# Seven half-size products for eight in the layers of six experts, with gathers, buffers and small steps in another order

## The chip, the cores and the metric

The kernel runs on one core of a Trainium2 chip. A core has a matrix engine (TensorE, in the profile PE for the products and PEld for the loading of their stationary operand), two engines for elementwise work (VectorE, DVE, and ScalarE, ACT), a programmable engine (GpSimd, POOL) that here issues the gathers and scatters, and a queue engine (SyncE, SP) that issues the plain transfers. Operands lie in the on-chip memory SBUF, results of TensorE in PSUM[...].

The metric is the device time of one launch in microseconds. The profile is a further, separately recorded execution.

## The reference

Two blocks are computed one after the other. The first is attention over 4 batches, 8 heads, 768 positions of 64 numbers, in which a query sees only the keys of the same hash bucket:

```python
q_bits = (np.einsum('bhsd,dk->bhsk', q, proj) > 0); k_bits = ...          # 6 bits
mask = q_bucket[:, :, :, None] == k_bucket[:, :, None, :]
scores = np.where(mask, q @ k.T / sqrt(64), -1e9)
attn = softmax(scores);  x = attn @ v          # then rearranged to 3072 tokens x 512
```

The second sends each of the 3072 tokens to one of 8 experts, the one with the largest cosine, and weighs the result with its softmax probability:

```python
expert_idx = np.argmax(logits, axis=1)                       # cosine of x and expert_emb
for e in range(8):                                            # D = 512, F = 1024
    h = np.maximum(x[mask] @ w1[e], 0.0)                      # first layer
    out[mask] = gate_w[mask, None] * (h @ w2[e])              # second layer
```

All inputs and outputs are float32. Nothing is rounded to a shorter type on the way, save the hash bits and masks, which are exact there.

## The kernel before

Attention goes in groups of three units; a unit is one block of 128 keys against 384 queries of two heads. TensorE makes the scores, ScalarE the exponentials, VectorE adds up the denominators, and TensorE multiplies with the values. Sixteen pairs of heads (`pr`) follow one another, four to a batch. After a pair, its result is divided by the denominators, squared for the norm and stored to a table `xd` in the main memory. The division and the sum of squares are partly on GpSimd:

```python
def add_squares(pr, rp):
    ...
    nc.scalar.activation(t[:], xs(b)[:, j], ACT.Square)
    if j > 0:
        nc.gpsimd.tensor_tensor(out=ssq[b][:], in0=ssq[b][:], in1=t[:], op=ALU.add)

def scale(pr):
    ...                                     # reciprocal, and its way through memory to rz
    nc.gpsimd.tensor_tensor(out=x, in0=x, in1=rz[:].rearrange("p s n -> p (s n)"), op=ALU.mult)
```

The last pair has no time for that way through memory. Its denominators are spread to all rows by a product with ones, and the reciprocal is taken of 384 columns:

```python
nc.tensor.matmul(ps[h * D : (h + 1) * D, 0, 0:SH], lhsT=ones[:, 0:D], rhs=acc[pr, s][:, h, :], ...)
...
nc.vector.reciprocal(out=z[:, s], in_=z[:, s])
```

After each batch the router counts its tokens into slots: each expert has three tiles of 128 tokens (`KT = 3`), and what does not fit goes to further tiles at the end. Two experts (`EARLY = 2`) get two tiles filled from the first three batches alone, so that TensorE has their 256 tokens to work on while the last batch is routed. The rows of a tile are gathered from `xd` by four indirect transfers and turned by VectorE:

```python
def fetch(pos, t, n, width=N + 1):
    ...
            for g in range(NQ):
                nc.gpsimd.indirect_dma_start(out=xg[:, g, :], ..., in_=xd[0 : width * NQ, :], ...)

def turn(parts, at):
    ...
        nc.vector.transpose(x[:, :, i * P : (i + 1) * P]..., xg[:]...)
```

The two layers of an expert (P = 128, ND = 4 blocks of the 512, NF = 8 blocks of the 1024):

```python
def hidden(i, xt, n, fs=range(NF)):
    for f in fs:
        ph = ps_h()
        for d in range(ND):
            nc.tensor.matmul(ph[:, 0:n], lhsT=w1s[i][:, d, f * P : (f + 1) * P], rhs=xt[:, d, 0:n], ...)
        nc.scalar.activation(ht[:, f, 0:n], ph[:, 0:n], ACT.Relu)

def second(i, j):
    py = ps_y()
    for f in range(NF):
        nc.tensor.matmul(py[:], lhsT=ht[:, f, j * P : (j + 1) * P], rhs=w2s[i][:, f, :], ...)
    return py

def result(i, tiles):
    for j, gate, src in tiles:
        send(weigh(second(i, j), gate), src)        # VectorE scales, GpSimd scatters
```

Each matmul of float32 stands in the profile as two instructions with a weight load each. The loop over the six experts with three tiles:

```python
for e in range(EARLY, E):
    i = e % NW                                       # NW = 3 sets of weights
    x, tiles = nxt
    if e == EARLY:
        late = [...]                                 # third tiles of the two early experts
    elif e + 1 < E:
        nxt = rows_of(e + 1)                         # 12 gathers, 3 turns, 3 gate gathers
    ...
    hidden(i, x, KT * P)
    ...
    bring1(i, e + NW)                                # next first-layer weights, 2 MB
    result(i, tiles)
    if e == EARLY:
        nxt = rows_of(e + 1)
        for o in range(EARLY):
            hidden(o, late[o][0], P); bring1(o, NW + o)
            result(o, late[o][1]);    bring2(o, NW + o)
        bring1(i, e + NW); bring2(i, e + NW)
    elif e + NW < E:
        bring2(i, e + NW)
```

After the loop follow the tiles beyond three, here two of 128 tokens.

Of the kernel before, what the change touches and what calls it, by code (L numbers as in the profile page):

```python
# [26 lines left out]
def kernel(  # L27
# [320 lines left out]
    NW = 3  # L348
# [6 lines left out]
    def bring1(i, e, **kw):  # L355
        nc.sync.dma_start(w1s[i][:], w1[bass.ds(e, 1)].rearrange("o (c p) f -> p (o c) f", p=P), **kw)
# [9 lines left out]
    def bring2(i, e, **kw):  # L366
        nc.sync.dma_start(w2s[i][:], w2[bass.ds(e, 1)].rearrange("o (c p) m -> p (o c) m", p=P), **kw)
# [5 lines left out]
    def fetch(pos, t, n, width=N + 1):  # L373
        parts = []
        for i in range(n):
            xg = xgs[taken[0] % len(xgs)]
            taken[0] += 1
            for g in range(NQ):
                nc.gpsimd.indirect_dma_start(  # L379
                    out=xg[:, g, :], out_offset=None, in_=xd[0 : width * NQ, :],  # L380
                    in_offset=bass.IndirectOffsetOnAxis(ap=pos[:, t + i, g : g + 1], axis=0))
            parts.append(xg)
        return parts
# [21 lines left out]
    ssq, lts = {}, {}  # L405


    def add_squares(pr, rp):
        b, j = pairs[pr]
        if j == 0:  # L410
            ssq[b] = ssq_
        t = ssq_ if j == 0 else rp.tile([P, S], F32, name="xsq", tag="junk", bufs=2)
        nc.scalar.activation(t[:], xs(b)[:, j], ACT.Square)  # L413
        if j > 0:
            nc.gpsimd.tensor_tensor(out=ssq[b][:], in0=ssq[b][:], in1=t[:], op=ALU.add)  # L415
# [13 lines left out]
    with ExitStack() as at:  # L429
# [52 lines left out]
        ld, feat, acc, av, zcs = {}, {}, {}, {}, {}  # L482
# [120 lines left out]
        def scale(pr):  # L603
# [5 lines left out]
            for h in range(2):  # L609
                nc.sync.dma_start(rz[h * D : (h + 1) * D],  # L610
                                  zd[pr].rearrange("(s h) n -> h s n", h=2)[h].unsqueeze(0).broadcast_to([D, 2, SH]))
            x = xs(b)[:, j]
            nc.gpsimd.tensor_tensor(out=x, in0=x, in1=rz[:].rearrange("p s n -> p (s n)"), op=ALU.mult)  # L613
# [11 lines left out]

        def scale_last(pr, s):
            b, j = pairs[pr]
            if s == 0:
                zcs[pr] = op.tile([P, 2, SH], F32, name="zl", tag="rz", bufs=1)
            z = zcs[pr]  # L630
            ps = banks()
            for h in range(2):
                nc.tensor.matmul(ps[h * D : (h + 1) * D, 0, 0:SH], lhsT=ones[:, 0:D], rhs=acc[pr, s][:, h, :],
                                 start=True, stop=True)
            nc.scalar.activation(z[:, s], ps[:, 0, 0:SH], ACT.Copy, bias=TINY * S)

        def scaled_last(pr, s):
            b, j = pairs[pr]
            z = zcs[pr]
            nc.vector.reciprocal(out=z[:, s], in_=z[:, s])  # L640
            x = xs(b)[:, j, s * SH : (s + 1) * SH]
            nc.vector.tensor_tensor(out=x, in0=x, in1=z[:, s], op=ALU.mult)
            nc.vector.tensor_tensor(out=z[:, s], in0=x, in1=x, op=ALU.mult)
# [55 lines left out]
        for u0 in range(0, U + G, G):  # L699
# [4 lines left out]
            if end and j == 2 and g == 3:  # L704
                run(99)
                listed = lists(slots, src[0][:], NS, rp)
            for u in range(u0, u0 + G):
                if u < U:
                    scores(u)
            for u in range(u0 - G, u0):  # L710
                if 0 <= u < U:
                    attend(u)
            if end and j == 2 and g == 3:
# [4 lines left out]
            if g == 0:  # L718
                if pr > 0:
                    sums(pr - 1)  # L720
                if j == 2 and end:
                    begin(b, spare(2 * E * NC))
# [7 lines left out]
            elif g == 1:  # L730
                prep_features(pr + 1, 1)
                if pr > 0:
# [18 lines left out]
            elif g == 2:  # L751
                prep_bits(pr + 1)
                if pr > 1:
                    store(pr - 2)
                if j == 2 and end:
                    run(99)
                    fill(b, spare(4 * NS))
                if j == 2 and b >= 0:
# [3 lines left out]
            else:  # L762
                if pr == 1:
# [3 lines left out]
                if j == 1 and b >= 0:  # L767
                    route(b, turn_logits(lts.pop(b), banks()[:, 0], rp), rp)
                if j == 3 and b >= 0 and not end:
                    run(99)  # L770
                    fill(b, spare(4 * NS))
                if j == 3 and end:
# [4 lines left out]
                    scaled_last(pr, 0)  # L777
                    store(pr - 1)
        scale_last(len(pairs) - 1, 1)
        scaled_last(len(pairs) - 1, 1)  # L780
        nc.vector.tensor_tensor(out=ssq[B - 1][:], in0=ssq[B - 1][:],
                                in1=zcs[len(pairs) - 1][:].rearrange("p s n -> p (s n)"), op=ALU.add)
# [124 lines left out]
    with ExitStack() as mo:  # L907
        mp = pool("mp", 1, mo)
        for i in range(1, NW):
            w1s.append(mp.tile([P, ND, F], F32, name=f"w1_{i}"))  # L910
            w2s.append(mp.tile([P, NF, DM], F32, name=f"w2_{i}"))
            bring1(i, i)
            bring2(i, i)
        xgt.extend(mp.tile([P, ND, KT * P], F32, name=f"xgt{i}") for i in range(NX))
# [13 lines left out]
        ps_x, ps_h, ps_y = turns(2, "ps_x"), turns(4, "ps_h"), turns(2, "ps_y")  # L928
        ht = mp.tile([P, NF, KT * P], F32, name="ht")
        ys = [mp.tile([P, DM], F32, name=f"y{i}") for i in range(3)]  # L930
        made = [0]

        def hidden(i, xt, n, fs=range(NF)):
            for f in fs:
# [4 lines left out]
                nc.scalar.activation(ht[:, f, 0:n], ph[:, 0:n], ACT.Relu)  # L939
# [19 lines left out]
        def result(i, tiles):  # L959
            for j, gate, src in tiles:  # L960
                send(weigh(second(i, j), gate), src)

# [64 lines left out]
        hidden(0, early_x[0], 2 * P, range(0, NF // 2))  # L1027
        lt = logits(b, ssq[b], ps_x(), sp)
        early_x.append(turn(early[1], 1))
        hidden(0, early_x[0], 2 * P, range(NF // 2, NF - 2))  # L1030
        l = turn_logits(lt, ps_x(), sp)
        hidden(0, early_x[0], 2 * P, range(NF - 2, NF))
        route(b, l, sp)
        result(0, early_g[0][0:1])
# [4 lines left out]
        last_ = second(0, 1)  # L1039
        hidden(1, early_x[1], 2 * P, range(0, 1))  # L1040
        fill(b, ps_x()[:, 0 : 4 * NS])
        half_ = lists(slots, src[1][:], NS, sp)
        hidden(1, early_x[1], 2 * P, range(1, 2))
# [108 lines left out]
```

## Time and profile before

| what | value |
|---|---|
| median of 3 timed runs | 748.25 us (746.86 to 752.0) |
| span of the profiled execution | 755.9 us |
| TensorE products, busy | 719.2 us, 95% of the span |
| VectorE busy | 355.4 us, 47% |
| ScalarE busy | 273.4 us, 36% |
| GpSimd busy | 223.9 us, 30% |
| last product of attention ends | about 361 us |
| last product of all ends | 742.5 us |
| moved by transfers | 87.56 MB |

The page gives the busy time of each engine, then the same in forty slices of 18.9 us as digits, then the costliest groups of instructions. A line of a group names the source line, the engine, the operation, output and inputs with their sizes and the count; behind the bar come busy time and mean duration of one, then the idle time of the engine just before these instructions. The timeline gives start, duration and group in order of time, with the idle time before it in brackets and what ended it. The durations of products overlap, since they are pipelined: what a product costs is the distance from start to start, which is the length of a row of products divided by their count.

### The profile page before, as it was taken

How to read it: one execution, taken by the hardware profiler on the slowest of the kernel's cores; microseconds unless marked ns; L12 is line 12 of the kernel's file. 1: busy time of each engine (PE TensorE's matmuls, PEld its weight loads, DVE VectorE, ACT ScalarE, POOL GpSimd, SP SyncE). 2: the span in 40 equal slices, each digit the busy share in tenths (PEclk: the TensorE clock that was granted, in tenths of full speed). 3: DMA queues.
4: the chain of work that ended last, by engine and by line, in shares of the span. 5: the costliest groups of instructions: out<-in, count | busy, mean ns of one | idle time of the engine just before them, and what ended most of it. 6: DMA issues, size and time to landing. Idle time of an engine off the chain costs nothing. (4 is left out here: it accounts for less than half of the span.)

```text
span 755.9 us, 10108 instructions
## 1 busy us (share of the span) xinstructions
PE 719.2 (95%) x3725; PEld 364.7 (48%) x3725; DVE 355.4 (47%) x648; ACT 273.4 (36%) x457; POOL 223.9 (30%) x222
## 2 busy tenths in 40 slices
PE   8999999999999999889599999799999999999992
PEld 5444444434444344344367455565454545545571
DVE  4877787889778978896723132101110100100100
ACT  2777676766666766655111010011010100101010
POOL 5011022112110111107613551716171524430250
PEclk9999999999999999999899999989999999999997
DMA  9634457764565566223393110489353534331010
GB/s 137 117 59 79 86 79 131 134 134 89 109 124 115 102 134 107 44 43 71 71 382 108 52 29 31 163 278 347 139 160 136 158 136 157 109 141 51 37 37 19
DMA packets 198171, 87.56 MB, mean 116 GB/s; under 512 B 171473, under 2 KB 179469, under 8 KB 198104
## 3 DMA queue, kind: packets, MB, share of 16 engines
q1 hardware_dynamic: 185272, 72.54, 39.2%
q0 software_dynamic: 6560, 13.41, 5.8%
q10 hardware_dynamic: 6272, 0.79, 1.0%
q8 instruction: 33, 0.54, 0.3%
q14 instruction: 34, 0.28, 0.1%
HBM read 86.50 MB, written 13.31 MB: 132 GB/s over the span
## 5 line engine op out<-in xcount | busy, mean ns | idle before, releaser
L945 PE MATMUL ps_y<-w,ht 128*128 128x512 f32 x416 | 180.6, 592 | 0.0
L557 ACT ACTIVATE p<-banks 128x768 f32<-128x768 f32 x192 | 151.8, 811 | 52.4 <-PE banks L554 47.0
L551 PE MATMUL banks<-qt,kt 64*128 64x384 f32 x768 | 163.7, 504 | 1.0 <-ACT p L557 0.6
L564 DVE TENSOR_TENSOR acc<-acc,p 128x768 f32<-128x768 f32 x128 | 146.6, 1145 | 17.9 <-ACT p L557 7.5
L939 ACT ACTIVATE ht<-ps_h 128x384 f32<-128x384 f32 (+2 forms) x96 | 37.3, 402 | 317.2 <-PE ps_h L937 238.2
L937 PE MATMUL ps_h<-xgt,w 128*128 128x384 f32 (+1 forms) x512 | 139.6, 434 | 0.0
L576 PE MATMUL av<-p,vt 128*64 128x385 f32 x768 | 138.3, 495 | 0.0
L945 PEld LDWEIGHTS ps_y<-w,ht 128*128 128x128 f32 x416 | 78.7, 190 | 95.0 <-issue 91.8
L937 PEld LDWEIGHTS ps_h<-xgt,w 128*128 128x128 f32 x512 | 87.4, 190 | 52.2 <-issue 2.9
L613 POOL TENSOR_TENSOR xT<-xT,rz 128x768 f32<-128x768 f32 x15 | 31.8, 2122 | 247.2 <-DMA rz<-zd 212.1
L379 POOL DMA_INDIRECT xg<-xd,pos x96 | 93.8, 977 | 33.3 <-issue 28.5
L551 PEld LDWEIGHTS banks<-qt,kt 64*128 64x128 f32 x768 | 65.5, 188 | 62.1 <-issue 35.1
L952 DVE TENSOR_SCALAR y<-ps_y,gg 128x512 f32<-128x512 f32 x26 | 19.5, 749 | 155.1 <-PE ps_y L945 144.8
L576 PEld LDWEIGHTS av<-p,vt 128*64 128x64 f32 x768 | 49.5, 136 | 76.5 <-issue 75.0
L956 POOL DMA_INDIRECT out_dram<-y,src x24 | 24.1, 1002 | 174.7 <-DVE y L952 142.7
L400 DVE STREAM_TRANSPOSE xgt<-xg 128x512 f32<-128x512 f32 x21 | 14.9, 712 | 126.9 <-DMA xg<-xd,pos 78.2
L554 PE MATMUL banks<-qb,kb 64*128 64x384 bf16 x384 | 64.0, 324 | 1.1 <-DVE kb L540 1.1
L937 PE MATMUL ps_h<-xge,w 128*128 128x256 f32 (+1 forms) x256 | 48.1, 346 | 11.7 <-issue 6.3
L937 PEld LDWEIGHTS ps_h<-xge,w 128*128 128x128 f32 x256 | 42.0, 205 | 18.2 <-issue 8.3
L561 DVE TENSOR_TENSOR acc<-p,p 128x768 f32<-128x768 f32 x32 | 34.2, 1068 | 11.8 <-ACT p L557 11.7
L554 PEld LDWEIGHTS <-kb 64*128 64x128 bf16 x384 | 19.6, 95 | 26.8 <-DVE kb L540 1.9
L415 POOL TENSOR_TENSOR ssq__163<-ssq__163,xsq 128x768 f32<-128x768 f32 x10 | 18.3, 1828 | 27.4 <-ACT xsq L413 27.3
(240 smaller groups left out, 399.8 us busy)
## 6 DMA issues: line engine op xcount, KB each, us to landing
w<-in_moe_w_dram SPq DMA_DIRECT2D x24, 2048.0 KB
qk<-in_q_dram SPq DMA_DIRECT2D x64, 96.0 KB
vt<-in_v_dram SPq DMA_DIRECT2D x16, 384.0 KB
xd<-xb SPq DMA_DIRECT2D x64, 96.0 KB
rz<-zd SPq DMA_DIRECT2D x30, 192.0 KB
qk<-in_k_dram SPq DMA_DIRECT2D x56, 96.0 KB
w<-in_moe_w_dram SPq DMA_DIRECT2D x8, 512.0 KB
xg<-xd,pos POOLq DMA_INDIRECT x96
```

The costliest lines, as they stand in the source:

```text
L379: nc.gpsimd.indirect_dma_start(out=xg[:, g, :], out_offset=None, in_=xd[0 : width * NQ, :], in_offset=bass.IndirectOffsetOnAxis(ap=pos[:, ...
L551: nc.tensor.matmul(ps[:, h, 0:SH], lhsT=kt[rows[h], c // HC, kc], rhs=qt[rows[h], s, :], start=True, stop=False)
L554: nc.tensor.matmul(ps[:, h, 0:SH], lhsT=kb[rows[h], c // HC, kc], rhs=qb[rows[h], s, :], start=False, stop=True)
L557: nc.scalar.activation(p[:, :, 0:SH], ps[:, :, 0:SH], ACT.Exp, scale=ESCALE)
L561: nc.vector.tensor_tensor(out=a[:], in0=pts[(u - 1) % NPT][:, :, 0:SH], in1=p[:, :, 0:SH], op=ALU.add)
L564: nc.vector.tensor_tensor(out=a[:], in0=a[:], in1=p[:, :, 0:SH], op=ALU.add)
L576: nc.tensor.matmul(ps[h * D : (h + 1) * D, 0 : SH + 1], lhsT=vt[:, h, c, :], rhs=p[:, h, 0 : SH + 1], start=(c == 0), stop=(c == NC - 1))
L613: nc.gpsimd.tensor_tensor(out=x, in0=x, in1=rz[:].rearrange("p s n -> p (s n)"), op=ALU.mult)
L937: nc.tensor.matmul(ph[:, 0:n], lhsT=w1s[i][:, d, f * P : (f + 1) * P], rhs=xt[:, d, 0:n], start=(d == 0), stop=(d == ND - 1))
L939: nc.scalar.activation(ht[:, f, 0:n], ph[:, 0:n], ACT.Relu)
L945: nc.tensor.matmul(py[:], lhsT=ht[:, f, j * P : (j + 1) * P], rhs=w2s[i][:, f, :], start=(f == 0), stop=(f == NF - 1))
L956: nc.gpsimd.indirect_dma_start(out=out[:, :], out_offset=bass.IndirectOffsetOnAxis(ap=src, axis=0), in_=y[:], in_offset=None, bounds_check ...
```

## The change

It concerns five things.

1. **Seven products for eight.** In the experts with three tiles (e = 2 to 7) a matrix product of halves, C = A B with A and B cut in two both ways, is made of seven half-size products and some sums instead of eight products (the scheme of Strassen in the form of Winograd). In the first layer this covers all 384 tokens (halves of 192); in the second layer 256 of the tokens (two tiles of 128), while the third tile goes the old way. VectorE makes the sums of the operands ahead and adds up the products from PSUM.
2. **Rows two experts ahead.** The gathers for expert e + 2 are issued when the first layer of e has ended, so that they run beside second layers.
3. **Pools.** Two sets of weights instead of three. The hidden layer, the outputs and the turned rows come first in their pool and the weights have one of their own; five banks of PSUM for the first layer instead of four, one instead of two for small products. The weights of expert 1 are asked for on ScalarE's queue.
4. **Slot steps.** The counting for the early experts in batch 3 (third of four) starts later and is spread differently between the score products; in the last batch the steps of the router are placed after other blocks of `hidden`.
5. **Division and squares.** Two elementwise operations of GpSimd go to VectorE; the last pair's reciprocal is taken of 6 columns instead of 384, with the denominators turned by small products.

The core of the diff:

```diff
-    NW = 3
+    NW = 2
...
-    def fetch(pos, t, n, width=N + 1):
+    def fetch(pos, t, n, width=N + 1, behind=None):
...
-            nc.gpsimd.tensor_tensor(out=ssq[b][:], in0=ssq[b][:], in1=t[:], op=ALU.add)
+            nc.vector.tensor_tensor(out=ssq[b][:], in0=ssq[b][:], in1=t[:], op=ALU.add)
...
-            nc.gpsimd.tensor_tensor(out=x, in0=x, in1=rz[:].rearrange("p s n -> p (s n)"), op=ALU.mult)
+            nc.vector.tensor_tensor(out=x, in0=x, in1=rzs.pop(pr)[:].rearrange("p s n -> p (s n)"), op=ALU.mult)
... scale_last, scaled_last
-                nc.tensor.matmul(ps[h * D : (h + 1) * D, 0, 0:SH], lhsT=ones[:, 0:D], rhs=acc[pr, s][:, h, :],
-                                 start=True, stop=True)
+                for i in range(HC):
+                    nc.tensor.matmul(ps[:, 0, h * HC + i : h * HC + i + 1], lhsT=acc[pr, s][:, h, i * P : (i + 1) * P],
+                                     rhs=ones[:, 0:1], start=True, stop=True)
...
+            nc.vector.reciprocal(out=z[:, s], in_=z[:, s])
...
+                    nc.tensor.matmul(ps[h * D : (h + 1) * D, 0, i * P : (i + 1) * P],
+                                     lhsT=z[:, s, h, i : i + 1].broadcast_to([P, D]), rhs=ident[:], start=True, stop=True)
... pools
+        ht = mp.tile([P, NF, KT * P], F32, name="ht")
+        ys = [mp.tile([P, DM], F32, name=f"y{i}") for i in range(3)]
+        xgt.extend(mp.tile([P, ND, KT * P], F32, name=f"xgt{i}") for i in range(NX))
         for i in range(1, NW):
-            w1s.append(mp.tile([P, ND, F], F32, name=f"w1_{i}"))
-            bring1(i, i)
+            wp = pool(f"wp{i}", 1, mo)
+            w1s.append(wp.tile([P, ND, F], F32, name=f"w1_{i}"))
...
-        ps_x, ps_h, ps_y = turns(2, "ps_x"), turns(4, "ps_h"), turns(2, "ps_y")
+        hb = [ps_m.tile([P, 512], F32, name=f"ps_h{i}") for i in range(5)]
+        ps_x, ps_y = turns(1, "ps_x"), turns(2, "ps_y")
... sums of operands (combine issues tensor_tensor on VectorE, `later` lets n of them go)
+        def sums_a(s, a11, a12, a21, a22, parts=1):      # 4 sums: of w1 (sw), of the hidden layer (sh)
+        def sums_b(t, b11, b12, b21, b22, parts=1):      # 4 sums: of w2 (tw, in 8 halves), of the rows (tx)
...
+        def seven(n, tm, mm, left, right, finish, between):
+            s1, u2, u4, ca, cb = (t[:, 0:n] for t in tm)
+            u3 = s1
+            def product(l, r, then):
+                ps = hb[hat[0] % 5][:, hat[0] // 5 % 2 * 256 :][:, 0:n]
+                hat[0] += 1
+                mm(ps, left[l], right[r])
+                later(then)
+                return ps
+            def plus(out, ps, s):
+                nc.vector.tensor_tensor(out=out, in0=ps, in1=s, op=ALU.add)
+            nc.scalar.copy(out=s1, in_=product(0, 0, 0))
+            plus(u2, product(5, 5, between[0]), s1)
+            plus(ca, product(1, 2, between[1]), s1)
+            finish(0, 0, ca)
+            plus(u4, product(4, 4, between[2]), u2)
+            d = product(6, 6, between[3])
+            plus(u3, d, u2)
+            plus(cb, d, u4)
+            finish(1, 1, cb)
+            plus(ca, product(7, 3, between[4]), u4)
+            finish(0, 1, ca)
+            plus(cb, product(3, 7, between[5]), u3)
+            finish(1, 0, cb)
+        def first_layer(i, x):
+            sums_b(tw, *(w2_part(i, j, k) for j in range(2) for k in range(2)), parts=2)
+            for f in range(NF // 2):
+                def mm(out, l, r):
+                    for d in range(ND // 2):
+                        nc.tensor.matmul(out, lhsT=l[:, d, f * P : (f + 1) * P], rhs=r[:, d, :], ...)    # 192 columns
+                def finish(j, k, c):
+                    acted[0] = nc.scalar.activation(ht[:, f + j * NF // 2, k * HT : (k + 1) * HT], c, ACT.Relu).ins
+                seven(HT, tmps[f % 2], mm, left, right, finish, (1, 0, 0, 0, 1, 0))
+            later(99)
+        def second_layer(i, tiles, upcoming, n0, between):
+            sums_a(sh, *left[0:4])
+            later(99)
+            x = upcoming()                    # turns rows of e + 1, gathers those of e + 2
+            py = second(i, j)                 # third tile, old way; ScalarE scales it
+            ...
+            later(n0)
+            def mm(out, l, r):
+                for f in range(NF // 2):
+                    nc.tensor.matmul(out, lhsT=l[:, f, :], rhs=r[:, f, :], ...)                          # 256 columns
+            seven(DM // 2, tmps[0], mm, left, right, finish, (1, 1, 1, 1, 0, 0))
+            later(99)
... the loop
         for e in range(EARLY, E):
             i = e % NW
-            hidden(i, x, KT * P)
+            first_layer(i, x)
...
+            done = acted[0]
+            def upcoming():
+                x = ready(e + 1, parts[e + 1])            # 3 turns, sums tx, sums sw
+                parts[e + 2] = fetch(pos[1][:], (e + 2) * KT, 2, behind=done)
...
-            result(i, tiles)
+            x, tiles = second_layer(i, tiles, upcoming, 4, between)
```

In the diff the third tiles of the two early experts now come before expert 2 and no longer after it.

## The prediction

> **What bounds the kernel now.** I read the page first: busy times, the forty slices, the costliest groups. Then the waits of TensorE, then TensorE's timeline from the end of attention on, where the change lies.
>
> ```profile
> PE 719.2 (95%) x3725; PEld 364.7 (48%) x3725; DVE 355.4 (47%) x648; ACT 273.4 (36%) x457; POOL 223.9 (30%) x222
> PE   8999999999999999889599999799999999999992
> DVE  4877787889778978896723132101110100100100
> ```
>
> TensorE is the bound nearly everywhere. The digits of VectorE show two different programs: up to slice 19 (361 us, attention) it is at seven to nine tenths, after that at one or two. So what VectorE is given in the expert part meets free time, what it is given in attention does not.
>
> TensorE's timeline of the expert part gives the prices (start, length, group, number):
>
> ```profile
> 404.08 10.61 PE L937 MATMUL ps_h<-xge,w 128*128 128x256 f32 x48
> 428.25 20.80 PE L937 MATMUL ps_h<-xgt,w 128*128 128x384 f32 x64
> 448.89 20.76 PE L945 MATMUL ps_y<-w,ht 128*128 128x512 f32 x48
> 469.49 7.31 PE L937 MATMUL ps_h<-xge,w 128*128 128x128 f32 x64
> 505.70 20.80 PE L937 MATMUL ps_h<-xgt,w 128*128 128x384 f32 x64
> ```
>
> The last product's tail overlaps the next row, so I take it off (0.17 us): 20.63/64 = 0.322 us per instruction of 384 columns, 20.6/48 = 0.429 for 512, 10.48/48 = 0.218 for 256, 7.15/64 = 0.112 for 128. The price goes with the columns, 0.83 to 0.87 ns each. A weight load stands in the groups with 190 ns, more than the 112 of the narrowest products, and still does not set the pace. For 192 columns, which the kernel before does not have, I put 0.165 us, between 128 and 256.
>
> The same timeline shows where TensorE is not held by its work:
>
> ```profile
> 360.46 0.87 PE L633 MATMUL banks<-acc,ones 128*64 128x384 f32 x4 [0.86 <-DVE acc L564]
> 362.49 7.14 PE L937 MATMUL ps_h<-xge,w 128*128 128x256 f32 x32 [1.17 <-issue]
> 377.33 5.37 PE L937 MATMUL ps_h<-xge,w 128*128 128x256 f32 x16 [5.24 <-ACT ht L939]
> 488.35 0.27 PE L937 MATMUL ps_h<-xge,w 128*128 128x128 f32 x1 [1.71 <-issue]
> 493.25 5.75 PE L937 MATMUL ps_h<-xge,w 128*128 128x128 f32 x33 [0.33 <-issue]
> ```
>
> From 362.5 to 505.7 pass 143.2 us. The products in it: two early experts with two tiles, 4 x 6.9 (hidden) + 4 x 6.9 (second) = 55.4; expert 2 41.3; two late tiles 2 x 14.0 = 28.0; router and logits about 3. Together 128. **Some 15 us are stalls and slow clock**, at two places: 372 to 381 (a hidden product waits for a ScalarE output that in turn waits for a store of attention, because the memory is reused) and 486 to 497.
>
> [...] behind the stall at 372 the granted clock over 370 to 380 is 0.69, and over 490 to 495 it is 0.50. A removed stall is therefore worth more than its length. [...] the running sum of attention takes 958 ns in the median but 1145 in the mean and up to 2545, and GpSimd's own product 2122 ns.
>
> **The change, part by part.**
>
> *Six experts.* Now each is 64 x 0.322 + 48 x 0.429 = 41.2 us. After: first layer 4 blocks x 7 products x 2 x 2 instructions = 112 x 0.165 = 18.5; third tile 16 x 0.429 = 6.9; second layer of two tiles 7 x 4 x 2 = 56 x 0.218 = 12.2. Sum 37.6 us. Saved 3.6 to 3.8 each, **22 us in six**, if TensorE stays the bound.
>
> *VectorE beside them.* One block of the first layer takes TensorE 28 x 0.165 = 4.6 us. VectorE has in it 7 additions of 192 columns [...] = 2.5, and two pieces of operand sums of 512 (691 ns) = 1.4, with some 40 ns between instructions (as in the router's steps, 0.24 from start to start at 0.20 long) 9 x 0.04 = 0.4: 4.3 us. That is 93% of TensorE's time. It fits, by little. The ring of five banks lets VectorE be some three us behind. Second layer: 4 sums of 512, 3 turns of 711 ns, 4 sums of 384 = 7.6 us against the third tile's 6.9; then 7 of 256 columns (424) and 4 of 1024 (1224) = 8.3 with gaps against 12.2. So VectorE is the bound nowhere on paper and near it in 24 blocks. [...] I charge **3 us**.
>
> *The stage from 362 to 506.* The order of the pools puts the hidden layer where the inputs of attention lay, of the same 30 KB per row of SBUF, whose readers are done; the store no longer holds it. That takes the 5.2 us and most of the slow clock after. The second stall goes with 12 MB of weights asked for in one burst (slices 26 and 27: 278 and 347 GB/s), while after the change only two sets wait at a time, each next to work on the other. Its cause I can't see fully: matmuls, ScalarE and VectorE all start again within two us, ScalarE after 12.4 us "remote". So I take **12 of 15 us** back.
>
> *Attention.* The page's waits of TensorE show 1.9 + 1.9 us for the slot steps of batch 3, and the clock halves there from 329 to 333, some 1.7 us more. Spreading the steps takes most: **4 us**. The last pair's denominators become 12 instructions of one column, twice, and 12 of 128 columns, twice: 48 x 0.112 = 5.4 us for 8 x 0.165 = 1.3; but the waits of 0.86 and 1.17 us at the end go too. I charge **2 us**. Division and squares add 15 + 12 instructions of 0.96 to VectorE, 24 us in 360, of which 291 are taken. [...] Nothing moves.
>
> *Gathers.* 18 indirect transfers per expert x 1.27 us (0.97 and 0.30 between) = 23 us, of 19 us of second layer. Some run over into the next first layer, but rows are wanted only an expert later: nothing on the path.
>
> *The rest* (two more tiles, 28 us, and the last 13 us after the final product) stays.
>
> Sum: -22 + 3 - 12 - 4 + 2 = -33 us.
>
> **The rivals.**
>
> *VectorE becomes the bound.* For it: 93% on paper, strict order, operands sums between additions, and chains to ScalarE and back. Against it: five banks, and sums done where TensorE is long. If each block took 5.2 us instead of 4.6, 24 x 0.6 = 14 us of the 22 go.
>
> *TensorE's releases come late.* In the kernel before, ScalarE's outputs of the experts were eight times released "remote", 36.2 us in total, up to 7.3 us late outside the stall, when TensorE had long gone on. It cost nothing there, as the hidden products had slack. The spacing is about 41 us of matmuls. If this goes by the number of instructions, 184 instead of 112 products per expert make it come oftener, and in the new scheme a late release stops VectorE, which cannot catch up at 93%. Nine times 0.5 to 3 us: I charge **4 us** to the sum.
>
> *The gain is only the stalls.* If 192 columns cost as much as the weight load (190 ns), the first layer would take 21.3 us, more than the 20.6 of before. Against it: 128 columns go at 112 ns with the same load.
>
> *Weights late with two sets.* First-layer weights of expert 2 are asked for about 21 us ahead of their use; 2 MB at the 350 GB/s of slice 27 take 6 us. Hidden.
>
> **Range and chances.** -33 + 4 = -29 us, so 748.25 - 29 = 719. With everything fitting and the whole of stalls and slot steps gone it is -22 - 15 - 6 = -43, that is 705. With VectorE as the bound (14 us back) and a new stall of 6 us it is about 739; that both come I hold for one in ten, so the range ends a little below. The 2% line is 733.3: it is missed when half of the expert saving and half of the stalls are lost together. Faster by over 2%: 0.83, within 2%: 0.13, slower: 0.04.
>
> **What would show it.** The pitch of 192-column products near 0.165 us in the timeline; an expert of about 38 us from first to first; VectorE at nine tenths in first layers and about eight in second ones. No 5 us wait of hidden products for ScalarE after 362, and a clock of 1 there. In attention the longest sum near 1.0 us and no mean above 1.0. Wrong I would be if waits of TensorE for VectorE's or ScalarE's reading of the five banks show in the first layers (the first rival), if these waits come in few long pieces at even distances (the second), or if the six experts start later than some 88 us after attention, because gathers or weights are late.

## The result, and the profile after

| | before | after |
|---|---|---|
| median of the timed runs, same chip | 747.86 us (746.86 to 752.0) | 722.39 us (721.9 to 725.15) |
| ratio | 1 | 0.9661, 95% interval 0.9622 to 0.97 |
| span of the profiled execution | 755.9 us | 719.9 us |

The change made the kernel 3.4% faster, 25.5 us; the prediction said 719. The two spans differ by 36 us, ten more than the times. The profiled execution of before took 757.69 us, more than any timed one, and it came to matter where the prediction read its stalls. One caution holds for all that follows: the runs went to several chips. On some the unchanged kernel before took 745 to 748 us, on others 757 to 760 us, so totals are compared only on one chip. The 3.4% belongs to the quicker ones; the changed kernel itself was not run on a slower one.

The busy times and two rows of slices of the page after answer to those shown of before:

```profile
PE 691.8 (96%) x4197; PEld 427.7 (59%) x4197; DVE 479.4 (67%) x984; ACT 307.5 (43%) x565; POOL 193.9 (27%) x202
PE   8999999999999999998899998999999999999992
DVE  5867787789778897698752022798867786866100
```

TensorE has 472 more instructions and 27 us less busy time. VectorE, which was at three tenths or less from slice 20 on (counted from 0), is now at six to nine tenths in slices 25 to 36, where the six experts are. TensorE's 5 and 7 of before, in slices 19 and 25, are gone.

For "where did the time come from" a trace of before on a chip of the quicker kind is needed. The experiment `b_pools` below supplies it: it is the kernel before with three allocations moved, and equal to it on the same chip (ratio 0.9996, 0.9981 to 1.0011). TensorE's timeline of it (start, length, group, number, idle time and its end):

```profile
360.43 7.14 PE L937 MATMUL ps_h<-xge,w 128*128 128x256 f32 x32 [1.17 <-ACT zl L635]
...
375.21 5.58 PE L937 MATMUL ps_h<-xge,w 128*128 128x256 f32 x16 [5.17 <-ACT ht L939]
...
426.33 20.80 PE L937 MATMUL ps_h<-xgt,w 128*128 128x384 f32 x64
446.97 20.76 PE L945 MATMUL ps_y<-w,ht 128*128 128x512 f32 x48
467.57 7.31 PE L937 MATMUL ps_h<-xge,w 128*128 128x128 f32 x64
...
495.60 20.80 PE L937 MATMUL ps_h<-xgt,w 128*128 128x384 f32 x64
...
704.23 7.31 PE L937 MATMUL ps_h<-xgt,w 128*128 128x128 f32 x64
```

The same timeline of the kernel after:

```profile
359.99 3.72 PE L976 MATMUL ps_h<-xge,w 128*128 128x256 f32 x16 [0.73 <-DVE xT L663]
...
446.77 0.81 PE L1091 MATMUL ps_h<-xgt,w 128*128 128x192 f32 x4
...
603.58 0.81 PE L1091 MATMUL ps_h<-xgt,w 128*128 128x192 f32 x4
...
640.73 0.81 PE L1091 MATMUL ps_h<-xgt,w 128*128 128x192 f32 x4
...
677.89 7.31 PE L976 MATMUL ps_h<-xgt,w 128*128 128x128 f32 x64
```

Row starts cut the span into stages. In `b_pools`, expert 2 lies inside the middle stage and takes 467.57 - 426.33 = 41.24 us. After, an undisturbed expert (from 603.58 to 640.73) takes 37.15 us.

| stage | before (`b_pools`) | after | difference |
|---|---|---|---|
| up to the first hidden product | 360.43 | 359.99 | -0.4 |
| early experts and their third tiles | 495.60 - 360.43 - 41.24 = 93.9 | 446.77 - 359.99 = 86.8 | -7.1 |
| six experts | 41.24 + (704.23 - 495.60) = 249.9 | 677.89 - 446.77 = 231.1 | -18.8 |
| the two further tiles and the end | 745.5 - 704.23 = 41.3 | 719.9 - 677.89 = 42.0 | +0.7 |
| sum | 745.5 | 719.9 | -25.6 |

The stall at 375 in `b_pools` is there as in before. The second one, near 490, is not: on this chip TensorE goes through 446.97 to 495.60 without a gap.

### The profile page after: what moved, and what is told of

Same layout as the page of the kernel before. It is cut to its first block, busy times and chain, and to the rows that moved or that the text cites. A ratio compares the mean times of both kernels' runs of the same rounds, so it can differ in the third digit from the quotient of the medians.

```text
span 719.9 us, 11583 instructions
## 1 busy us (share of the span) xinstructions
PE 691.8 (96%) x4197; PEld 427.7 (59%) x4197; DVE 479.4 (67%) x984; ACT 307.5 (43%) x565; POOL 193.9 (27%) x202
## 4 chain that ended last, share of the span: by engine, by line
PE 79%; DVE 7%; POOL 4%; issue 3%; DMA 3%; ACT 1%; SPq 0%; POOLq 0%; DVEq 0%; ACTq 0%
PE ps_h L1091 15%; PE banks L560 15%; PE av L585 15%; PE ps_y L984 11%; PE ps_h L1120 10%; PE ps_h L976 6%; PE banks L563 4%; POOL xg L379 3%; DVE acc L573 2%; PE banks L538 2%; PE banks L602 1%; DMA proj<-in_proj_dram 1%; DVE kt L517 1%; DMA out_dram<-y,osrc 0%; DMA qk<-in_k_dram 0%
## 5 line engine op out<-in xcount | busy, mean ns | idle before, releaser
L573 DVE TENSOR_TENSOR acc<-acc,p 128x768 f32<-128x768 f32 x128 | 122.1, 954 | 20.7 <-ACT p L566 11.0
L1066 DVE TENSOR_TENSOR tm<-ps_h,tm 128x192 f32<-128x192 f32 (+1 forms) x210 | 72.2, 368 | 56.5 <-PE ps_h L1120 30.4
L984 PE MATMUL ps_y<-w,ht 128*128 128x512 f32 x224 | 98.4, 593 | 0.0
L984 PEld LDWEIGHTS ps_y<-w,ht 128*128 128x128 f32 x224 | 41.9, 190 | 47.4 <-issue 47.1
L1095 ACT ACTIVATE ht<-tm 128x192 f32<-128x192 f32 x96 | 32.6, 362 | 74.7 <-DVE tm L1066 74.7
L1091 PE MATMUL ps_h<-tx,xT 128*128 128x192 f32 x288 | 56.0, 332 | 2.6 <-DVE xT L1026 2.6
L991 DVE TENSOR_SCALAR y<-ps_y,gg 128x512 f32<-128x512 f32 x8 | 6.0, 751 | 70.7 <-PE ps_y L984 70.7
L1091 PEld LDWEIGHTS ps_h<-tx,xT 128*128 128x128 f32 x288 | 49.3, 194 | 2.9 <-DVE xT L1026 2.9
L978 ACT ACTIVATE ht<-ps_h 128x128 f32<-128x128 f32 (+1 forms) x48 | 15.0, 313 | 74.9 <-PE ps_h L976 73.3
L1091 PE MATMUL ps_h<-xgt,w 128*128 128x192 f32 x192 | 39.5, 328 | 0.0
```

Of the source, the lines that this page charges most:

```text
L573: nc.vector.tensor_tensor(out=a[:], in0=a[:], in1=p[:, :, 0:SH], op=ALU.add)
L1066: nc.vector.tensor_tensor(out=out, in0=ps, in1=s, op=ALU.add)
L1091: nc.tensor.matmul(out, lhsT=l[:, d, f * P : (f + 1) * P], rhs=r[:, d, :], start=(d == 0), stop=(d == ND // 2 - 1))
L1095: acted[0] = nc.scalar.activation(ht[:, f + j * NF // 2, k * HT : (k + 1) * HT], c, ACT.Relu).ins
```

## The experiments

**The kernel before once more** (`b_again`), to learn what the 755.9 us of its first profile were.

> The kernel before, unchanged, profiled once more. The first profile's span (755.9 us) lies some 8 to 10 us above what the timed runs leave for a span (747.9 us less about 2). Theory 1: the stall at 486 to 497 us in the late tiles, with ScalarE released "remote" after 12.4 us, belongs to that one execution; then this span is 745 to 749 us, the rows from 469.5 to 505.7 us (36.2) become about 28, and the stall at 372 us before ScalarE's first hidden outputs is still there (5 us and half clock). Theory 2: the stall belongs to the kernel; then this span is again near 755 us.

Measured: 756.24 us beside 757.11 for before on that chip. ScalarE's timeline of `b_again` at the place of the second stall:

```profile
491.56 0.61 ACT L939 ACTIVATE ht<-ps_h 128x128 f32<-128x128 f32 x3 [12.49 <-remote]
```

The late release of 12.49 us comes at the same place as in the first profile (12.41), and is absent in `b_pools`, on a chip where the kernel takes 745 us. The span is near 755 us again, as the second theory said, though not on every chip. The first profile looks like one of the slower kind; its chip isn't known.

**Which layer gives what** (`a_eight`, `a_first8`, `a_second8`): the kernel after with the old eight products in both layers, in the first alone, in the second alone.

```diff
-            sums_b(tx, ...); sums_a(sw, ...)                 # a_eight, a_first8: no sums of rows and of w1
-            for f in range(NF // 2): ... seven(HT, ...)
+            for f in range(NF):
+                hidden(i, x, KT * P, range(f, f + 1)); later(1)
-            sums_a(sh, *left[0:4]); ... seven(DM // 2, ...)   # a_eight, a_second8: no sums of ht and of w2
+            for j in range(2):
+                py = second(i, j); later(2)
+                nc.scalar.activation(two[j][:], py[:], ACT.Copy, scale=tiles[j][1][:, 0:1])
```

> The changed kernel with eight products again in both layers of the six experts; pools, order of gathers, slot steps, division and reciprocals stay changed. Theory 1, the gain is the matrix products saved: an expert goes from 37.15 us back to 41.2, six make +24.3 us, less some 6 us that the first expert loses now on its operand sums, so 739 to 743 us, that is 5 to 9 us under the kernel before, which is the share of all the other parts. Theory 2, the gain is mostly stalls removed by pools and order: 728 to 732 us.

> Eight products in the first layer only, seven stay in the second. By the price per column 6 x (20.6 - 18.2) = +14.4 us, less up to 5 us of the first expert's stall, which is a stall on the operand sums of w1: 732 to 737 us. If the first layer's seven products were already held by VectorE, undoing them would cost less: 724 to 730 us.

> Eight products in the second layer's two tiles only, seven stay in the first layer. By the price per column 6 x (20.6 - 18.95) = +9.9 us, less 1.2 us of wait for the hidden layer's sums in the first expert: 730 to 733 us. Together with the run before it in this list it should add up to the run with eight in both, within 2 us, if the two layers don't share a limit.

Measured, beside 757.11 for before: 765.87, 789.66 and 760.54 us, that is 1.0115 (1.0082 to 1.0148), 1.042 (1.039 to 1.045) and 1.0051 (1.0029 to 1.0072). All are slower than before and far above the 730 to 743 us expected, although TensorE has fewer large products than in before or as many; the late releases told of below lie in them, so the totals say little of the layers. The last expert of the loop is free of stalls in all three, and it can be read. Its rows in the timeline of `a_eight`:

```profile
680.19 20.80 PE L976 MATMUL ps_h<-xgt,w 128*128 128x384 f32 x64
...
721.43 0.83 PE L976 MATMUL ps_h<-xgt,w 128*128 128x128 f32 x6
```

and in those of `a_first8` and `a_second8`, the expert's first row and the first of the next work:

```profile
699.08 20.80 PE L976 MATMUL ps_h<-xgt,w 128*128 128x384 f32 x64
...
738.68 1.05 PE L976 MATMUL ps_h<-xgt,w 128*128 128x128 f32 x8
```

```profile
681.46 0.81 PE L1090 MATMUL ps_h<-xgt,w 128*128 128x192 f32 x4
...
720.26 0.94 PE L976 MATMUL ps_h<-xgt,w 128*128 128x128 f32 x7
```

So 41.24 us with eight products in both (the 41.24 of before), 39.60 with seven in the second layer, 38.80 with seven in the first, 37.15 with both. Taking the seven out of the first layer costs 2.45 us, out of the second 1.65; together 4.10 of 4.09. The parts add, which would not be expected if VectorE were the bound.

**How near VectorE is** (`a_dve2`, `a_dve4`): two or four further additions of 512 columns, of no use, per block of the first layer.

```diff
+                if n == HT and k in (1, 5):                  # a_dve4: (1, 2, 3, 5)
+                    nc.vector.tensor_tensor(out=scratch[:], in0=left[0][:, 0], in1=left[0][:, 1], op=ALU.add)
```

> The changed kernel with two more VectorE sums of 512 columns in each of the 24 blocks of the six first layers, written to a tile nobody reads. Prediction's theory, VectorE at 93% of a block (each instruction costs its duration and 40 ns): two more make 4.3 + 1.45 = 5.75 us for 4.55 of TensorE, so 24 x 1.2 = +29 us. New theory, from the changed kernel's trace, where instructions that follow at once start 0.27 us (192 columns) and 0.60 us (512) apart: 7 x 0.27 + 2 x 0.60 = 3.1 us, with two more 4.3 us, still under 4.55: 0 to +3 us.

> The same with four more sums per block. New theory: 3.1 + 4 x 0.60 = 5.5 us for 4.55 of TensorE: +0.95 x 24 = +23 us, less what the ring of banks buffers, so +15 to +25 us. Prediction's theory: 4.3 + 2.9 = 7.2, +2.65 x 24 = +64 us.

Measured, beside 759.66 for before: 774.88 us, 1.0235 (1.0177 to 1.0292), and 790.67, 1.0401 (1.0362 to 1.0439), again with late releases in both. The busy times of a first layer free of stalls decide (window; its length; busy us of PE, PEld, DVE, ACT, POOL; clock). The kernel after, first and second layer of the last expert but one:

```profile
603.58:621.78 18.20, 18.20 (x113) 18.20 (x112) 13.53 (x35) 6.12 (x19) 6.30 (x6) 1.00 0.43 150
621.78:640.73 18.95, 18.95 (x74) 13.68 (x73) 14.09 (x24) 3.21 (x7) 14.21 (x12) 1.00 0.46 154
```

`a_dve2`, first layer of the last expert:

```profile
683.83:702.03 18.20, 18.20 (x114) 18.20 (x113) 17.03 (x42) 6.42 (x19) 3.18 (x3) 1.00 0.41 141
```

`a_dve4`, the same:

```profile
700.80:721.75 20.95, 20.53 (x113) 17.89 (x112) 19.24 (x45) 5.85 (x18) 3.34 (x3) 1.00 0.34 123
```

VectorE is 74% busy (13.53 of 18.20), not 93%. With two more additions it is 94% busy and TensorE loses nothing in this layer; with four the layer grows by 2.75 us, and VectorE sets the pace. The total of `a_dve2` does not follow: it is 8.9 us above that of `a_slot` below (765.97 us on the same chip), where VectorE has no such additions. In both, late releases disturb the layers ahead of the last expert. The four first layers between the first expert and the last take 85.6 us together in `a_dve2` (20.71 to 22.06 each), 80.2 in `a_slot` (19.07 to 21.34) and 82.3 in `a_pool`, against 18.20 each undisturbed. The slack is thus shown for undisturbed layers alone; the rest fits the second rival, in which a VectorE at 93% cannot catch up after a late release. The timeline of VectorE in the kernel after shows why the prediction's price was too high:

```profile
623.59 0.69 DVE L1026 TENSOR_TENSOR sh<-sh,ht 128x512 f32<-128x512 f32 x1
624.20 0.68 DVE L1026 TENSOR_TENSOR sh<-ht 128x512 f32<-128x512 f32 x1
624.80 0.68 DVE L1026 TENSOR_TENSOR sh<-ht,sh 128x512 f32<-128x512 f32 x1
```

Each lasts 0.68 us, but they start 0.605 us apart: the durations overlap, as those of products do. Two additions of 192 columns in a row together take 0.61 to 0.62 us, so 0.26 apart at 0.36 long. By these distances a block is estimated at 7 x 0.27 + 2 x 0.60 = 3.1 us of 4.55, with two more sums 4.3, with four 5.5. Of the last, 5.24 are seen (20.95/4).

**Two attention parts undone** (`a_pool`: squares and division on GpSimd again; `a_slot`: slot steps of batch 3 at their old places).

```diff
-            nc.vector.tensor_tensor(out=ssq[b][:], ...); nc.vector.tensor_tensor(out=x, in0=x, ...)
+            nc.gpsimd.tensor_tensor(out=ssq[b][:], ...); nc.gpsimd.tensor_tensor(out=x, in0=x, ...)     # a_pool
+            if end and j == 2 and g == 3:                                                               # a_slot
+                run(99); listed = lists(slots, src[0][:], NS, rp)
-                    if g == 1 and u == u0 + 1: begin(...)
-                    elif g == 2: run(2 if u < u0 + 2 else 99)
```

> The changed kernel with the division and the sum of squares of attention back on GpSimd, in their new places in the order. Theory 1 (prediction): [...] within 1.5 us of the changed kernel, running sums again at a mean of about 1.1 us. Theory 2: with VectorE late, the slot steps and the last pair come later; +2 to +5 us.

> The changed kernel with the slot steps of batch 3 in the old order. Theory 1 (prediction): waits of 1.9 + 1.9 us and 1.7 us of half clock come back, against 0.8 + 1.2 us now: +2 to +5 us. Theory 2: with GpSimd's products gone from attention VectorE is no longer late there, and the order does nothing: 0 to +1 us.

Measured on the chip of `a_dve2`: 768.12 us, 1.0126 (1.0084 to 1.0167), and 765.97, 1.0099 (1.0063 to 1.0134). The totals again hold late releases; the traces up to 350 us do not. The groups of the running sum, first the kernel after, then `a_pool` (count, busy us, mean ns, idle before):

```profile
L573 DVE TENSOR_TENSOR acc<-acc,p 128x768 f32<-128x768 f32 x128 | 122.1, 954 | 20.7 <-ACT p L566 11.0
```

```profile
L573 DVE TENSOR_TENSOR acc<-acc,p 128x768 f32<-128x768 f32 x128 | 146.2, 1142 | 26.9 <-ACT p L566 16.7 <-ACT few L590 0.5
```

So these two operations on GpSimd alone make the running sums 24.1 us longer. Up to the hash products of the last pair TensorE notices nothing of it: they begin at 323.4 us in `b_pools` and 323.1 in the kernel after. TensorE's waits up to 352 us (in total, times, longest) and the busy times from 320 us on (columns as above), `b_pools` and then after, tell what the attention part is worth:

```profile
PE banks L338 <- DVE half__3158 L330: 2.3, 1, 2.3
PE av L323 <- DVE col L316: 1.9, 1, 1.9
```

```profile
320.00:350.00 30.00, 25.78 (x176) 11.15 (x174) 22.96 (x45) 15.56 (x23) 11.88 (x10) 0.94 0.26 42
```

```profile
PE banks L192 <- DVE ssq__163 L424: 2.5, 3, 1.0
PE banks L338 <- DVE half__3160 L330: 1.2, 1, 1.2
...
PE av L323 <- DVE col L316: 0.8, 1, 0.8
```

```profile
320.00:350.00 30.00, 28.05 (x201) 12.07 (x199) 24.87 (x61) 18.38 (x29) 13.42 (x12) 1.00 0.35 59
```

The waits for slot steps fall from 4.2 to 2.0 us, and the clock from 320 to 350 us rises from 0.94 to 1.00, which is 1.8 us more. A new wait of 2.5 comes: the router's product with the squares now waits, in three batches, for the sum of squares, which stands in VectorE's queue. `a_pool` hasn't this wait. In `a_slot` the slot waits stay at 2.0 (0.8 and 1.2): with all else of the change, their old places cost nothing more. In `a_pool` they are 2.7 (1.2 and 1.5), so either part without the other takes most of the 4.2.

`a_pool` pays elsewhere. Its ScalarE, then TensorE:

```profile
347.87 0.84 ACT L417 ACTIVATE xsq<-xT 128x768 f32<-128x768 f32 x1 [8.00 <-POOL xT L626]
```

```profile
349.46 1.65 PE L560 MATMUL banks<-qt,kt 64*128 64x384 f32 x4 [5.44 <-ACT p L566]
```

In the new order the division on GpSimd stands behind eight gathers and starts at 346.02 us; in the kernel before it went ahead of them (333.99, the first gather at 340.27). The last pair's small products begin at 360.61 us, in `a_slot` at 352.17. With the new order, the division on VectorE instead of GpSimd is thus worth some 8 us of this trace. The total does not show it, since `a_pool` has no late release of ten us just behind, as `a_slot` has.

**The last pair's reciprocal undone** (`a_last`).

```diff
-                for i in range(HC):
-                    nc.tensor.matmul(ps[:, 0, h * HC + i : h * HC + i + 1], lhsT=acc[pr, s][:, h, i * P : (i + 1) * P], rhs=ones[:, 0:1], ...)
+                nc.tensor.matmul(ps[h * D : (h + 1) * D, 0, 0:SH], lhsT=ones[:, 0:D], rhs=acc[pr, s][:, h, :], ...)
```

> The changed kernel with the last pair's old reciprocals (two of 384 columns, 2.5 us each) and their old places. Prediction: the new way costs TensorE 4 us more products and takes 2 us of waits away, so undoing it gains 2 us. From the changed trace its products take only 4 x 1.2 us (1.36 for twelve of one column, 0.72 for twelve of 128) and the hidden products start 2.5 us earlier than before; and the logits now come 3.6 us behind them, which with the old reciprocals would wait: undoing it costs +1 to +5 us.

Measured: 722.21 us, ratio 0.9695 (0.9668 to 0.9721) to 745.37 for before. Its timeline:

```profile
356.22 3.69 PE L967 MATMUL ps_h<-xge,w 128*128 128x256 f32 x16 [1.56 <-ACT zl L649]
...
363.71 0.83 PE L192 MATMUL ps_x<-xT,enT 128*32 128x384 f32 x2 [2.38 <-DVE xT L656]
...
448.60 0.81 PE L1082 MATMUL ps_h<-xgt,w 128*128 128x192 f32 x4
```

Without the 48 small instructions hidden products begin 3.8 us earlier, but the logits wait 2.38 us for the reciprocal of 384 columns, and expert 2 begins at 448.60 where the kernel after has 446.77. Up to there this part gains 1.8 us instead of costing 2. In these two traces it is lost again at once: expert 2 takes 41.50 us in `a_last` and 43.17 in the kernel after, with the same waits, but a clock of 1.00 against 0.96 over 447 to 490 us. The spans are 719.7 and 719.9 us, and the intervals of the ratios (0.9695 and 0.9661) overlap, so a gain in the total is not shown.

**The place of the hidden layer alone** (`b_pools`): the kernel before, with `ht`, the outputs and the turned rows allocated ahead of the weights in the same pool.

```diff
         mp = pool("mp", 1, mo)
+        ht = mp.tile([P, NF, KT * P], F32, name="ht")
+        ys = ...; xgt.extend(...)
         for i in range(1, NW):
             w1s.append(mp.tile([P, ND, F], F32, name=f"w1_{i}"))
```

> The kernel before with only the order of the tiles in its pool changed: hidden layer, outputs and turned rows first, weights behind them. Theory 1: the wait at 372 us is for a store of attention whose memory the hidden layer reuses; it goes with its half clock, 5.2 + 1.7 us: 740 to 742 us. Theory 2: the new place only hands the wait to the weights, which are then late for expert 1: within 2 us of the kernel before.

Measured: 745.87 us, ratio 0.9996 (0.9981 to 1.0011). The 5.17 us wait stays, as shown above, so the order is not what removes it. ScalarE's timeline and that of the queue of plain transfers in `b_pools`:

```profile
374.77 1.21 ACT L939 ACTIVATE ht<-ps_h 128x256 f32<-128x256 f32 x4 [14.98 <-DMA xd<-xb]
```

```profile
354.87 17.69 SPq L623 DMA_DIRECT2D xd<-xb  x9
374.75 0.39 SPq L356 DMA_DIRECT2D w<-in_moe_w_dram  x1
```

Output of the hidden layer and weights are released in the same moment, 374.75 and 374.77, by the last store of attention. It looks as if everything in one pool waits for all that lay in its memory. The change also gives the weights a pool of their own, and there `ht` is written from 362.02 on. That this second half does it is a guess from what is left; it wasn't tried alone and is not shown.

**A version that mends the first expert** (`better`). The kernel after loses time when it enters the new scheme (VectorE's timeline):

```profile
446.97 0.75 DVE L991 TENSOR_SCALAR y<-ps_y,gg 128x512 f32<-128x512 f32 x1 [13.26 <-PE ps_y L984]
447.64 1.22 DVE L1026 TENSOR_TENSOR xT<-w 128x1024 f32<-128x1024 f32 x1
...
475.23 2.87 DVE L1178 TENSOR_TENSOR ocol<-ohit,tok 128x600 bf16<-128x600 f32 x4
478.01 0.69 DVE L1026 TENSOR_TENSOR sh<-ht 128x512 f32<-128x512 f32 x1
```

and TensorE waits for it:

```profile
450.17 0.92 PE L1091 MATMUL ps_h<-tx,xT 128*128 128x192 f32 x4 [2.58 <-DVE xT L1026]
...
479.48 1.99 PE L1120 MATMUL ps_h<-xT,sh 128*128 128x256 f32 x8 [1.22 <-DVE sh L1026]
```

VectorE idles 13.26 us for a scaling that stands ahead of the sums of `w1`, though the sums need nothing of it. Later the list of the further tiles stands ahead of the sums of the hidden layer. The first expert takes 489.94 - 446.77 = 43.17 us instead of 37.15; beside the waits it has a clock at half behind the first (0.50 from 452 to 454 us; the mean over 447 to 490 is 0.96).

```diff
+        ctl, ocol = beyond_tiles()                     # ahead of the third tiles of the early experts
         ... for o in range(EARLY):
+            if o == EARLY - 1:
+                later(99)                              # the sums of w1, ahead of the last scaling
             send(weigh(py, ...))
-            if e == EARLY:
-                ctl, ocol = beyond_tiles()
```

> The changed kernel with two moves: the operand sums of w1 for the first of the six experts go before the scaling of the last late tile in VectorE's order, and the steps that count the tiles beyond three go before the late tiles, where VectorE is idle. Theory: TensorE's waits of 2.6 us (with 1.7 us of half clock and some slow start behind it) and of 1.2 us go: 716 to 718 us, -0.6 to -0.9%. Rival: the sums then wait for w1 and the scaling behind them, or the beyond steps make the late rows' turn late: within 1 us of the changed kernel.

Measured: 715.95 us, ratio 0.9600 (0.9583 to 0.9618), beside 722.21 for `a_last` on the same chip. The first expert starts without a wait:

```profile
446.51 0.81 PE L1091 MATMUL ps_h<-xgt,w 128*128 128x192 f32 x4
447.16 0.81 PE L1091 MATMUL ps_h<-tx,xT 128*128 128x192 f32 x4
```

It ends at 483.66, 37.15 us later. It is the fastest version, 4.0% ahead of before.

**The changed kernel once more** (`a_again`).

> The changed kernel once more, beside the kernel before on the same chip. The kernel before took 745 to 748 us in two calls and 757 to 760 in two others. Where it takes 745 to 748 here, all theories expect 722 us and a ratio near 0.966. Where it takes 757 to 760, they part. Theory of late releases (the prediction's second rival, which holds on such a chip alone): about 760 to 766 us, a ratio of 1.00 to 1.01, with a wait of some 10 us before the first hidden product of expert 2, single products more than 1 us apart at 416 to 437 us, and gaps of 1 to 2 us in first layers. Theory that the variants run there lost their gain by their own edits: about 733 us, a ratio near 0.966, and none of those gaps.

Measured: 722.45 us, ratio 0.9666 (0.9632 to 0.97) to 745.82. The chip was of the quicker kind, so the result is confirmed there, and the question of the other chips stays.

**The late releases.** All seven variants of the changed kernel on the chips with 757 to 760 us have them, six of them with 10.4 to 13.4 us at the same place, the reciprocal of the last pair; `a_slot` is as near to the changed kernel as `a_last` is. Its timelines, TensorE and then ScalarE:

```profile
352.17 1.50 PE L649 MATMUL banks<-ones,acc 128*128 128x1 f32 x12
367.08 1.55 PE L660 MATMUL banks<-ident,zl 128*64 128x128 f32 x12 [13.42 <-DVE zl L652]
...
427.26 1.01 PE L981 MATMUL ps_y<-w,ht 128*128 128x512 f32 x1 [1.08 <-issue]
429.36 1.01 PE L981 MATMUL ps_y<-w,ht 128*128 128x512 f32 x1 [1.09 <-issue]
```

```profile
366.63 0.18 ACT L651 ACTIVATE zl<-banks 128x6 f32<-128x6 f32 x1 [10.63 <-remote]
```

The small products at L649 are done at 353.7, ScalarE is let go at 366.6, and TensorE stands for 13.42 us. Around 428 TensorE makes one product per 2.1 us and waits for nothing that the profile shows. "Remote" marks a release whose origin the profile doesn't show; in the program ScalarE waits here for TensorE's products. In before the worst such place, near 490, costs five to six us of waits of TensorE (5.1 in the first profile, 5.7 in `b_again`); in the variants the places lie where TensorE itself needs the answer. The traces of the kernel after, `a_last`, `better`, `a_again` and `b_pools` have no remote release at all from 340 us on. Nearly the same code thus behaves differently by chip; what makes the releases late there stays open. Of the changed kernel on such a chip only its near variants tell: `a_slot` and `a_pool` were 1.0 and 1.3% slower than before there.

## Why the prediction was right, and where it wasn't

Its sum, term by term, against the stages of the two quick traces and, where the attention part and the last pair are to be told apart, that of `a_last`:

| term | predicted | measured |
|---|---|---|
| six experts, seven for eight | -22 | 6 x 4.09 = -24.5 |
| VectorE beside them | +3 | steady experts 0; first expert +6.0 |
| attention: slot steps | -4 | -4.2 (hidden products at 356.22 in `a_last`, 360.43 in `b_pools`) |
| last pair, and stage of the early experts | +2 - 12 | +3.8 - 7.1, about -3.4 |
| late releases | +4 | 0 on this chip |
| the rest | 0 | about +0.5 |
| sum | -29 | -25.6 |

*Seven for eight.* The mechanism and nearly the size were right. Products of 192 columns go at 18.20/112 = 0.1625 us (0.165 predicted), an expert takes 37.15 us (37.6), and the weight load, 190 ns in the median there, does not set the pace, so the third rival is out.

*VectorE beside them.* The mis-sized step is the price of a block, 4.3 us: it added 40 ns to each instruction's length. The lengths were the author's estimate and hold in the trace of after: 354 ns in the mean for 192 columns, 423 for 256, 682 to 692 for 512, 1215 to 1222 for 1024. The trace of before leads to the same price: it shows 558 ns for 384 columns and 951 for 768, the line through the two gives 361 for 192 and 689 for 512, and 7 x 0.361 + 2 x 0.689 + 9 x 0.04 is 4.3 us. But the instructions overlap: their starts are 605 ns apart for 512 columns and 260 to 270 for 192, the latter with one operand in PSUM. By the prediction's own price `a_dve2` would need 4.3 + 2 x 0.73 = 5.8 us per block of 4.55; its undisturbed layer lost nothing. The first rival is out as a lasting bound. What VectorE did cost, 6.0 us, is order and not load: 2.58 and 1.22 us of waits at the entry of the scheme, and a clock of 0.50 behind the first. No step of the prediction looked at that first expert. The 3 us were thus too high for a reason that didn't occur, and too low for one that did.

*The stage from 362 to 506.* "Some 15 us are stalls" was true of the profiled execution and not of the timed ones. The trace of before on a quicker chip has 495.60 - 360.43 = 135.2 us there for 128 us of products, so 7 us to gain, and the stage is 7.1 shorter. The pools alone do not give that: in `a_last`, which has the new pools and the old reciprocal, the stage is 448.60 - 356.22 = 92.4 us, only 1.5 under `b_pools`, because the wait for the reciprocal and a slow clock behind it (0.83 over 360 to 370 us, 1.00 after) take the place of the stall. The other 5.6 come with the last pair's part, whose small products cost 3.8 ahead of the stage. Two waits lay side by side, and the prediction priced them as separate terms. The signs were in the given numbers: 757.69 us for the profiled run, 752.0 at most for the timed ones, and a stall in which all engines start again at once. The cause named for the first stall, the order of the pools, fails by `b_pools`; something that the change does beyond the order removes it.

*Attention.* The 4 us came, in the place named: 2.2 of waits and 1.8 of slow clock. That the spreading of the steps brings them is not borne out: `a_slot` has the old places and no more waits. "Nothing moves" set the 24 us of additions against running sums shorter by (1145 - 958) x 128 = 24 us, and both came: the additions take 14.3 + 9.2 = 23.5 us, the sums 122.1 us in the kernel after and 146.2 in `a_pool`. It holds for TensorE up to 323 us, where the squares' 2.5 us of new waits are made up for; behind it, by `a_pool`, some 8 us hang on the division. The last pair was charged 2 us and gains 1.8 up to expert 2, by the trace of `a_last`. A running sum takes 954 ns in the mean after and 1142 in `a_pool`; why it lasts longer beside GpSimd's operations was not shown.

*Late releases.* The second rival exists, strongly, on another kind of chip. On the chips of the measured result its 4 us were not lost.

So the hit at 722 rests on one good mechanism, the seven products, on a good size for the slot steps, and on errors that cancel by luck: 6.6 us too much credited for the stalls and the last pair together, and a first expert that cost 3 us more than the charge; against them 4 us charged for releases that did not come and 2.5 us too little credited for steady experts.

## What to carry to other kernels

Before taking a stall's length out of a profile, set the profiled run against the timed ones: a stall that makes the profile longer than all of them isn't there to be gained. When a new scheme gives an idle engine work, price back-to-back instructions by the distance of their starts, and then look at the first pass apart from the steady ones: here the order of one queue cost 6 us at the entry, and two moved steps took it back. When two waits lie side by side, price them together: removing one alone may show the other. A few extra instructions of no use on the suspected engine tell its slack, where nothing else disturbs the stretch.

## What the runs showed of the hardware that was not expected

VectorE's float32 additions overlap in the kernel after: 512 columns last 0.68 us and start 0.605 us apart, 192 columns 0.36 and 0.26. The same kernel differs by 12 us between chips (745.37 and 757.11), with releases of ScalarE after up to 12.49 us of idle time on the slower ones (`b_again`), marked "remote", at places that recur from run to run; their cause is open.
